# A seven-batch x ring in a tuned attention kernel: memory found by smaller buffers, and a smaller lead for the K waves

## The chip, the cores and the metric

One core of one Trainium2 chip. The metric is the device time of one execution in microseconds (us), as the median of several runs. Two versions are called the same when they differ by less than 2%.

## The reference

Two independent attention problems, A and B, of the same size. Their outputs stand side by side.

```python
# x [16,144,448], k_cache and v_cache [16,16,512,256], wq [448,4096], wo [4096,448], all bf16
q = (x @ wq).reshape(16, 144, 16, 256).transpose(0, 2, 1, 3)
scores = jnp.einsum("bhqd,bhkd->bhqk", q, k_cache) * (256 ** -0.5)
p = softmax(scores)
o = jnp.einsum("bhqk,bhkd->bhqd", p, v_cache)
out = o.transpose(0, 2, 1, 3).reshape(16, 144, 4096) @ wo
# ... the same for B; concatenate([a, b], axis=-1)
```

## The kernel before

The kernel calls one (problem, batch, head) a *unit*. There are 512, of about 2 us each: units 0 to 255 are A, 256 to 511 are B. TensorE does for each unit its Q projection (ahead of time), the scores S (three units ahead), P·V, a matmul with ones that sums the rows of P, and pieces of the output projection.

All loads but a few at the start go through one DMA queue, issued by SyncE. A K *wave* brings the K of 16 units at once by a transposing DMA (4.19 MB), into a ring of 32 units. A V load brings two units (512 KB), into a ring of nine. x comes in groups of two or four batches, into a ring of six batches. The weights wq and wo of B replace those of A around unit 256. The order of the queue is planned when the program is built:

```python
NV, NX = 9, 6
MARGIN, HOLD, K_FIX = 1.0, 1.0, 2.4
# ...
for XG, (g0, g1) in enumerate(X_GROUPS):      # groups of x, by batch: (2,6) (6,10) ... (18,20) ...
    load(first_q[g0], (g1 - NX) * H - lq(NT) if g1 > NX else s_min, 1.3 + 0.55 * (g1 - g0), t_load_x, XG)
for W, (u0, u1) in enumerate(WAVES):
    last = u1 - 1 - KR
    load(u0 - ls(u0), last - ls(last) + 1 if last >= 0 else s_min, K_FIX + 0.97 * (u1 - u0), t_load_k, W)
```

The arguments of `load` are the step that needs the transfer, the first step at which its buffer is free, and the time that the planner allows for it. `K_FIX` is the fixed part of that time for a K wave: a smaller one lets the wave be placed later against V loads.

The sum of the rows of P goes through three engines. GpSimd adds twice, VectorE folds the upper half of the partitions onto the lower, and TensorE sums with ones, once for two units:

```python
def t_presum(U):
    def e1(g):      # GpSimd, first add
        return g.tensor_tensor(pp_sb[:, :, :], pt_sb[:, psl, 0:2, :], pt_sb[:, psl, 2:4, :], op=ALU.add)
    # ...
    dst, key = (ps_sb[:, sl, :], (("ps", sl), U)) if U < P0 else (p2_sb[:, :], ("p2", U))
    def e2(g):      # GpSimd, second add
        return g.tensor_tensor(dst, pp_sb[:, 0, :], pp_sb[:, 1, :], op=ALU.add)

def t_halves(U):    # VectorE, the fold
    def e(v):
        return v.tensor_tensor(ps_sb[p0:p0 + 64, sl, :], p2_sb[0:64, :], p2_sb[64:128, :], op=ALU.add)
```

VectorE also copies Q out of PSUM (`qt_sb<-qp_ps`) and normalises P·V (`ring<-ot_ps,rinv_sb`). The scheduler adds the waits that reads and writes of the same buffer make necessary.

## Time and profile before

| | before |
|---|---|
| median, lowest, highest | 1050.94, 1048.6, 1051.23 us (3 runs) |
| profiled run | 1052.7 us, of which the profile spans 1050.9: slower than each of the timed runs |
| TensorE, VectorE, ScalarE, GpSimd busy | 1031.5, 797.3, 794.2, 631.9 us |
| longest wait of TensorE | 6.0 us, for the K wave of unit 288 |

The lines themselves are in the prediction below. Three notes on reading them. In a list of waits the three numbers are the sum in us, how often it happened and the longest. In a timeline a line is its start, its length, the engine with its line of code, the operation, the tiles, and in brackets how long the engine stood idle just before it and what released it. A line of a window has its length, the busy time and instruction count of the five engines (TensorE, its weight loads, VectorE, ScalarE, GpSimd), then the granted clock of TensorE (1.00 is full), the DMA share and GB/s.

### The profile page before, as it was taken

What the parts mean: (1) busy time and instruction counts of PE and PEld (TensorE: products, weight loads), DVE (VectorE), ACT (ScalarE), POOL (GpSimd) and SP (SyncE); (2) the same over time, 40 slices, a digit from 0 to 9 for tenths busy, and PEclk for the clock granted to TensorE, in tenths of its full rate; (3) what the DMA queues carried; (4) which work ended last, traced back from release to release, by engine and by line L of the source; (5) the groups of instructions that cost most, each with busy time, mean ns of one, the idle gap of its engine ahead of it and who ended that gap; (6) DMA issues with size and microseconds to landing.
All of it is one profiled execution on the core that took longest, in us unless ns stands there. A gap on an engine that the chain in (4) does not pass through costs nothing.

```text
span 1050.9 us, 32573 instructions
## 1 busy us (share of the span) xinstructions
PE 1031.5 (98%) x12432; PEld 877.9 (84%) x12432; DVE 797.3 (76%) x2042; ACT 794.2 (76%) x2368; POOL 631.9 (60%) x1030
## 2 busy tenths in 40 slices
PE   8999999999999999999999799999999999999997
PEld 8999888888788888888887688888888888888885
DVE  5776787778777787787677668788787777788874
ACT  5877677778777777888766568787887777788785
POOL 3654556666566666666655456666666666666673
PEclk9999999999999999999999999999999999999999
DMA  9999999999999999999999999999999999999970
GB/s 320 362 325 318 302 268 248 283 282 291 295 294 303 273 283 238 296 286 298 260 295 337 250 288 292 290 282 294 273 264 270 295 285 294 264 273 287 288 235 13
DMA packets 590884, 294.11 MB, mean 280 GB/s; under 512 B 501440, under 2 KB 515904, under 8 KB 590720
## 3 DMA queue, kind: packets, MB, share of 16 engines
q1 hardware_dynamic: 590240, 291.72, 111.5%
q8 instruction: 100, 1.64, 0.6%
q14 instruction: 64, 0.52, 0.1%
q10 hardware_dynamic: 480, 0.23, 0.1%
HBM read 161.74 MB, written 4.13 MB: 158 GB/s over the span
## 4 chain that ended last, share of the span: by engine, by line
PE 90%; DMA 8%; SPq 2%; issue 0%; ACT 0%; DVE 0%; DVEq 0%; ACTq 0%
PE ot_ps L1219 23%; PE s_ps L1163 23%; PE qp_ps L1132 22%; PE op_ps L1335 18%; DMA kt_sb<-in_B_k_cache_dram 3%; DMA kt_sb<-in_A_k_cache_dram 2%; PE ot_ps L1235 2%; DMA wq_sb<-in_A_wq_dram 1%; DMA v_sb<-in_B_v_cache_dram 1%; PE qp_ps L1083 1%; PE s_ps L1083 1%; SPq L1053 1%; DMA wq_sb<-in_B_wq_dram 1%; PE qp_ps L1335 1%; DMA v_sb<-in_A_v_cache_dram 0%; SPq L981 0%
## 5 line engine op out<-in xcount | busy, mean ns | idle before, releaser
L1183 POOL TENSOR_TENSOR pp_sb<-pt_sb 128x288 f32<-128x288 bf16 x512 | 380.5, 743 | 305.1 <-ACT pt_sb L1173 290.3
L1173 ACT ACTIVATE pt_sb<-s_ps 128x288 bf16<-128x288 f32 x1024 | 364.5, 408 | 182.0 <-PE s_ps L1163 176.3
L1163 PE MATMUL s_ps<-qt_sb,kt_sb 128*128 128x144 bf16 x4096 | 340.3, 226 | 6.4 <-DMA kt_sb<-in_B_k_cache_dram 5.8
L1219 PE MATMUL ot_ps<-pt_sb,v_sb 128*128 128x144 bf16 x4096 | 340.2, 226 | 2.6 <-DMA v_sb<-in_B_v_cache_dram 1.4
L1163 PEld LDWEIGHTS s_ps<-qt_sb,kt_sb 128*128 128x128 bf16 x4096 | 288.3, 98 | 55.2 <-issue 6.3
L1256 ACT ACTIVATE rinv_sb<-ln_sb 64x144 f32<-64x144 f32 x928 | 298.3, 321 | 24.2
L1132 PE MATMUL qp_ps<-xt_sb,wq_sb 128*128 128x288 bf16 (+1 forms) x2368 | 300.8, 270 | 1.9 <-DMA wq_sb<-in_A_wq_dram 1.2
L1335 PE MATMUL op_ps<-wo_sb,ring 128*128 128x448 bf16 x1120 | 286.0, 353 | 0.0
L1188 POOL TENSOR_TENSOR p_sb<-pp_sb 128x144 f32<-128x144 f32 x464 | 227.3, 490 | 92.4 <-DVE ps_sb L1197 53.3
L1219 PEld LDWEIGHTS ot_ps<-pt_sb,v_sb 128*128 128x128 bf16 x4096 | 274.3, 98 | 3.6 <-DVE ps_sb L1197 3.1
L1132 PEld LDWEIGHTS qp_ps<-xt_sb,wq_sb 128*128 128x128 bf16 x2368 | 212.2, 98 | 77.1 <-DVE run_sb L1286 1.1
L1146 DVE CAST qt_sb<-qp_ps 128x576 bf16<-128x576 f32 x216 | 163.4, 757 | 140.1 <-PE qp_ps L1132 139.9
L1197 DVE TENSOR_TENSOR ps_sb<-p_sb 64x144 bf16<-64x144 f32 x464 | 241.5, 520 | 34.9 <-POOL p_sb L1188 16.1
L1271 DVE TENSOR_TENSOR ring<-ot_ps,rinv_sb 128x288 bf16<-128x288 f32 (+2 forms) x640 | 237.6, 387 | 18.6 <-ACT rinv_sb L1256 13.6
L1286 DVE TENSOR_REDUCE run_sb<-ot_ps 128x1 bf16<-128x144 f32 x560 | 144.9, 300 | 41.7 <-ACT rinv_sb L1243 26.6
L1335 PEld LDWEIGHTS op_ps<-wo_sb,ring 128*128 128x128 bf16 x1120 | 94.0, 98 | 20.7 <-issue 0.5
L1243 ACT ACTIVATE ln_sb<-ot_ps 128x144 f32<-128x144 f32 x232 | 67.9, 293 | 33.6 <-PE ot_ps L1235 26.8
L1235 PE MATMUL ot_ps<-ps_sb,ones 128*128 128x144 bf16 x280 | 63.3, 226 | 0.0
L1145 DVE CAST qt_sb<-qp_ps 128x288 bf16<-128x288 f32 x80 | 36.0, 450 | 4.1 <-PE qp_ps L1132 3.2
L1091 ACT ACTIVATE kt_sb<-qp_ps 128x512 bf16<-128x512 bf16 x48 | 28.9, 602 | 0.9 <-PE qp_ps L1083 0.9
L1235 PEld LDWEIGHTS ot_ps<-ps_sb,ones 128*128 128x128 bf16 x280 | 27.4, 98 | 1.1 <-DVE ps_sb L1197 1.1
L1188 POOL TENSOR_TENSOR ps_sb<-pp_sb 128x144 bf16<-128x144 f32 x48 | 23.5, 489 | 6.9 <-PE ot_ps L1235 0.3
(37 smaller groups left out, 162.5 us busy)
## 6 DMA issues: line engine op xcount, KB each, us to landing
v_sb<-in_A_v_cache_dram SPq DMA_DIRECT2D x128, 512.0 KB, 7.4
v_sb<-in_B_v_cache_dram SPq DMA_DIRECT2D x128, 512.0 KB, 7.5
v_sb<-in_A_k_cache_dram SPq DMA_DIRECT2D x22, 512.0 KB, 10.1
out_dram<-ost_sb SPq DMA_DIRECT2D x36, 112.0 KB, 6.3
wo_sb<-in_A_wo_dram SPq DMA_DIRECT2D x8, 448.0 KB, 7.4
wo_sb<-in_B_wo_dram SPq DMA_DIRECT2D x8, 448.0 KB, 8.3
wq_sb<-in_B_wq_dram SPq DMA_DIRECT2D x4, 768.0 KB, 10.1
wq_sb<-in_A_wq_dram SPq DMA_DIRECT2D x3, 768.0 KB, 9.0
```

Source lines behind the costliest of these rows:

```text
L1132: ins = t.matmul(acc, lhsT=wq_sb[:, kc, c0:c0 + 128], rhs=xt_sb[:, kc, xo:xe + 1:max(xe - xo, 1), :], start=(kc == 0), stop=(kc == 3))
L1146: return v.tensor_copy(qt_sb[:, a:b + 1:b - a, :, :], qp_ps[:, :, 0:2 * SQ].rearrange("p e (u q) -> p u e q", u=2))
L1163: ins = t.matmul(s_ps[bank][:, (c % 2) * SQ:(c % 2 + 1) * SQ], lhsT=kt_sb[:, 2 * c + dc, ko:ko + 128], rhs=qt_sb[:, qsl, dc, :], start=(dc ...
L1173: return a.activation(pt_sb[:, psl, 2 * k:2 * k + 2, :].rearrange("p b q -> p (b q)"), s_ps[bank][:, 0:2 * SQ], AF.Exp, scale=DH ** -0.5)
L1183: return g.tensor_tensor(pp_sb[:, :, :], pt_sb[:, psl, 0:2, :], pt_sb[:, psl, 2:4, :], op=ALU.add)
L1188: return g.tensor_tensor(dst, pp_sb[:, 0, :], pp_sb[:, 1, :], op=ALU.add)
L1197: return v.tensor_tensor(ps_sb[p0:p0 + 64, sl, :], p2_sb[0:64, :], p2_sb[64:128, :], op=ALU.add)
L1219: ins = t.matmul(ot_ps[ob][:, dc * SQ:(dc + 1) * SQ], lhsT=v_sb[:, vsl, j, c * DH + dc * 128:c * DH + (dc + 1) * 128], rhs=pt_sb[:, sl, c, ...
L1256: return a.activation(rinv_sb[p0:p0 + 64, sl, :], ln_sb[h0:h0 + 64, :], AF.Exp, scale=-1.0)
L1271: ins = v.tensor_tensor(ring[:, 2 * h:2 * h + 2, r0:r0 + q1 - q0], ot_ps[ob][:, 0:2 * SQ].rearrange("p (c q) -> p c q", c=2)[:, :, q0:q1], ...
L1286: return v.tensor_reduce(run_sb[:, k, j:j + 1], ot_ps[ob][:, 2 * SQ:3 * SQ], axis=AX.X, op=op)
L1335: ins = t.matmul(acc[0:m, 0:D], lhsT=ring[:, c, col0:col0 + m], rhs=wo_sb[:, c, :], start=(c == op_first), stop=(c == op_last))
```

## The change

The intent: give x a ring of seven batches, so that x groups can be issued sooner and need not queue up beside K and V; issue one group 40 units sooner still; and place K waves with a smaller lead. The memory for the seventh batch comes from other buffers.

```diff
-    NV, NX = 9, 6
+    NV, NX = 9, 7
-    MARGIN, HOLD, K_FIX = 1.0, 1.0, 2.4
+    MARGIN, HOLD, K_FIX = 1.0, 1.0, 2.0
-        ps_sb = sb("ps_sb", [128, NPS, SQ], BF16)          # NPS = 2
+        ps_sb = sb("ps_sb", [128, SQ], BF16)
-        p2_sb = sb("p2_sb", [128, SQ], F32)
...      (short reductions in groups of 20 instead of 28, their results in bf16, a flag moved into another buffer)
-            dst, key = (ps_sb[:, sl, :], (("ps", sl), U)) if U < P0 else (p2_sb[:, :], ("p2", U))
+            dst, key = ps_natural(U) if U < P0 else (pp_sb[:, 0, :], ("pp", ("p2", U)))
...
-                return v.tensor_tensor(ps_sb[p0:p0 + 64, sl, :], p2_sb[0:64, :], p2_sb[64:128, :], op=ALU.add)
+                return v.tensor_tensor(ps_sb[p0:p0 + 64, :], pp_sb[0:64, 0, :], pp_sb[64:128, 0, :], op=ALU.add)
...
-                load(first_q[g0], (g1 - NX) * H - lq(NT) ...
+                load(first_q[g0] - (40 if g0 == Bn + 2 else 0), (g1 - NX) * H - lq(NT) ...
```

So the second add now writes into `pp_sb`, its own input, and the fold reads it there: the first add of the next unit must wait until the fold is done.

More of the change, by code (lines that the diff above doesn't have):

```diff
@@ L802, in bass_concat_heads__mha_block_cached__gqa_block_cached__near_ridge_kernel @@
     WARM = 32
-    NQT, NPT, NPS, NRI, NOST = 11, 4, 2, 2, 2
+    NQT, NPT, NRI, NOST = 11, 4, 2, 2
     RS = 3
@@ L812, in bass_concat_heads__mha_block_cached__gqa_block_cached__near_ridge_kernel @@
     NCK = P0 + (NT - P0) // 2
-    NRUN = max(n for n in range(1, 33) if NCK % n == 0)
+    NRUN = max(n for n in range(1, 21) if NCK % n == 0)
     assert P0 % KG == 0
@@ L841, in bass_concat_heads__mha_block_cached__gqa_block_cached__near_ridge_kernel @@
         pp_sb = sb("pp_sb", [128, 2, SQ], F32)
-        ps_sb = sb("ps_sb", [128, NPS, SQ], BF16)
+        ps_sb = sb("ps_sb", [128, SQ], BF16)
         rinv_sb = sb("rinv_sb", [128, NRI, SQ], F32)
-        p2_sb = sb("p2_sb", [128, SQ], F32)
         ln_sb = sb("ln_sb", [128, SQ], F32)
         run_sb = sb("run_sb", [128, 2, NRUN], BF16)
-        runs_sb = sb("runs_sb", [128, 2, NCK // NRUN], F32)
+        runs_sb = sb("runs_sb", [128, 2, NCK // NRUN], BF16)
         ost_sb = sb("ost_sb", [128, NOST, D], BF16)
-        stat = sb("stat", [128, 4], F32)
-        flag_sb = sb("flag_sb", [128, 4], I32)
+        stat = sb("stat", [128, 8], F32)
+        flag_sb = stat.bitcast(I32)[:, 4:8]
         qp_ps = ps("qp_ps", [128, 2, 512], F32)
@@ L957, in e @@
                     sems["wo%d" % wg], 16)
-            over = [(("xn", g), 1) for g in range(NX) if pr == 0 and wg in x_rows(g)[2]]
+            over = [(("xn", g), 1) for g in X_AT if pr == 0 and wg in x_rows(g)[2]]
             S.add(SP, e, writes=[(("wo", wg), pr)] + over, dma_sem="wo%d" % wg, name="wo%d.%d" % (pr, wg))
@@ L997, in x_rows @@
             n = SQ // XR
-            c0 = NWO - (NX - g) * n
+            c0 = NWO - (len(X_AT) - g) * n
             return n, wo_sb[0:XR, c0:c0 + n, :], sorted(set(c // WOG for c in range(c0, c0 + n)))
@@ L1176, in t_s, with ps_natural @@
                       name="ex%d.%d" % (U, k))
+        def ps_natural(U):
+            if U % 2:
+                return ost_sb[:, 1, 0:SQ], (("ost", 1), ("ps", U))
+            return ps_sb[:, :], ("ps", U)
         def t_presum(U):
             psl = U % NPT
-            sl = U % NPS
             def e1(g):
@@ L1191, in t_halves @@
         def t_halves(U):
-            sl = U // 2 % NPS
             p0 = U % 2 * 64
             def e(v):
-                return v.tensor_tensor(ps_sb[p0:p0 + 64, sl, :], p2_sb[0:64, :], p2_sb[64:128, :], op=ALU.add)
-            S.add(DVE, e, reads=[("p2", U)], writes=[(("ps", sl), ("p", U // 2)), ("halves", U)], name="hv%d" % U)
+                return v.tensor_tensor(ps_sb[p0:p0 + 64, :], pp_sb[0:64, 0, :], pp_sb[64:128, 0, :], op=ALU.add)
+            S.add(DVE, e, reads=[("pp", ("p2", U))], writes=[("ps", ("p", U // 2)), ("halves", U)], name="hv%d" % U)
         def ring_cols(pr, b):
@@ L1228, in t_sum @@
             if U < P0:
-                rhs, keys = ps_sb[:, U % NPS, :], [("ones", 0), (("ps", U % NPS), U)]
-            else:
-                sl = U // 2 % NPS
-                rhs, keys = ps_sb[:, sl, :], [("ones", 1), (("ps", sl), ("p", U // 2))]
+                rhs, key = ps_natural(U)
+                keys = [("ones", 0), key]
+            else:
+                rhs, keys = ps_sb[:, :], [("ones", 1), ("ps", ("p", U // 2))]
             def e(t):
@@ L1451, in load_list @@
             for XG, (g0, g1) in enumerate(X_GROUPS):
-                load(first_q[g0], (g1 - NX) * H - lq(NT) if g1 > NX else s_min, 1.3 + 0.55 * (g1 - g0), t_load_x, XG)
+                load(first_q[g0] - (40 if g0 == Bn + 2 else 0), (g1 - NX) * H - lq(NT) if g1 > NX else s_min, 1.3 + 0.55 * (g1 - g0), t_load_x, XG)
             for W, (u0, u1) in enumerate(WAVES):
```

## The prediction

> **What bounds the kernel now.** I read the page's busy shares first, then the list of waits of TensorE, then the chain of waits around the longest of them, then the DMA queue's own timeline with the landing time of every transfer.
>
> ```profile
> PE 1031.5 (98%) x12432; PEld 877.9 (84%) x12432; DVE 797.3 (76%) x2042; ACT 794.2 (76%) x2368; POOL 631.9 (60%) x1030
> ...
> PE s_ps L1163 <- DMA kt_sb<-in_B_k_cache_dram: 5.8, 1, 5.8
> PE ot_ps L1219 <- DMA v_sb<-in_B_v_cache_dram: 1.4, 2, 1.2
> PE ot_ps L1219 <- DMA v_sb<-in_A_v_cache_dram: 1.2, 1, 1.2
> PE qp_ps L1132 <- DMA wq_sb<-in_A_wq_dram: 1.2, 2, 0.9
> ```
>
> TensorE is busy 98% of 1050.9 us, and the change takes no matmul away. So only its waits can be won. Comparing each matmul's start-to-start time with the usual one for its form (62 ns for 144 columns, 123 for 288, 189 for 448) gives all that TensorE loses after its first matmul: 14.5 us. After the ramp the losses that matter, by position, are 0.5 at 181 us (K wave for unit 80), 1.4 at 266 (V of unit 120), 0.7 at 521 (first wq of B), 1.3 at 561 (V of unit 268), 6.0 at 598 (K wave for unit 288), 0.4 at 758 (V of unit 364). All are waits for a transfer.
>
> ```profile
> 573.05 4.24 SPq L1053 DMA_DIRECT2D v_sb<-in_B_v_cache_dram  x4
> 577.33 24.43 SPq L1039 DMA_TRANSPOSE kt_sb<-in_B_k_cache_dram  x1
> 601.80 0.58 SPq L1364 DMA_DIRECT2D out_dram<-ost_sb  x1
> ...
> 597.42 0.23 PE L1235 MATMUL ot_ps<-ps_sb,ones 128*128 128x144 bf16 x1
> 597.49 0.54 PE L1335 MATMUL op_ps<-wo_sb,ring 128*128 128x448 bf16 x2
> 603.87 1.12 PE L1163 MATMUL s_ps<-qt_sb,kt_sb 128*128 128x144 bf16 x8 [5.84 <-DMA kt_sb<-in_B_k_cache_dram]
> 604.78 1.16 PE L1219 MATMUL ot_ps<-pt_sb,v_sb 128*128 128x144 bf16 x8
> 605.74 1.70 PE L1335 MATMUL op_ps<-wo_sb,ring 128*128 128x448 bf16 x4
> ...
> 598.00:610.00 12.00, 6.16 (x46) 4.65 (x46) 2.49 (x7) 2.73 (x9) 2.09 (x4) 0.72 1.11 288
> ```
>
> The reader is to see three things. A transposed K wave of 16 units (4.19 MB) holds the one queue for 24 us: nothing behind it is issued until it is nearly done. Four V loads go out just before it. And after the 6 us gap the next matmuls run slow (8 in 1.12 us instead of 0.66) until about 608.4 us: some 2.8 us more. The stall costs 8.8 us, over half of all that can be won.
>
> **What the Trainium skill says.** "TensorE: Matmul & The Clock Gate", section "Why this matters for your kernels": keep idle gaps under about 3 us, else the clock falls to half. The trace agrees: 0.72 granted clock in the window above, and no slow matmuls after the 1.4 us gaps. "DMA: Bandwidth & Descriptors", section "Latency and other measured facts", gives a transposing DMA 261 GB/s; here a wave lands 17.1 us after the transfer ahead of it (median of those with a queue), 245 GB/s, against 1.35 us for a V load of 512 KB, 388 GB/s. "SBUF — State Buffer", section "SBUF: two separate sides": a VectorE operation with two SBUF inputs and a GpSimd operation that reads SBUF exclude each other, and the loser waits. The trace agrees, with the fold of the row sums on VectorE:
>
> ```profile
> 704.37 0.73 POOL L1183 TENSOR_TENSOR pp_sb<-pt_sb 128x288 f32<-128x288 bf16 x1 [0.76 <-ACT pt_sb L1173]
> 704.49 0.78 DVE L1197 TENSOR_TENSOR ps_sb<-p_sb 64x144 bf16<-64x144 f32 x1
> 705.35 0.49 POOL L1188 TENSOR_TENSOR p_sb<-pp_sb 128x144 f32<-128x144 f32 x1 [0.24 <-DVE ps_sb L1197]
> 705.87 0.30 DVE L1197 TENSOR_TENSOR ps_sb<-p_sb 64x144 bf16<-64x144 f32 x1
> ```
>
> **The change, part one: smaller buffers.** The room for a seventh batch comes from one ps_sb instead of two and from folding in place in pp_sb. Each engine's instructions keep their order, but for 8 more short reductions on VectorE (14 groups of 20 instead of 10 of 28; at about 0.1 us each, nothing). New waits: GpSimd's first add of unit U+1 waits for VectorE's fold of U, and an even fold for the sum matmul of the pair before. In the window above the add at 704.37 would wait for the fold at 704.49, which now runs alone in 0.30 us: it starts at about 704.83, and its fold ends at 706.5 instead of 706.17. VectorE then has 0.5 us of reductions before the Q eviction at 707.13, ahead of which it idles 0.45 us today. The 0.3 us fit into that. The sum matmul that the even fold waits for ended at 701.94, before the fold's start at 702.08. So TensorE sees nothing. VectorE gains: 464 folds of 520 ns mean become about 305 ns, some 100 us less busy, off the path. I put +0.2 us on it.
>
> **Part two: the order of the queue.** The queue's order in both built programs shows few moves: K waves 2 and 16 ahead of one V load each, K wave 3 ahead of x group 1 and two V loads; ten V loads (units 120, 252, 362, 394 and six others) ahead of a K wave; V loads of units 266, 330 and 378 behind one; x groups 2, 3, 4 and 7 one place earlier, each now ahead of a K wave that it followed. The x group issued 40 units sooner moves from unit 220 to 204.
>
> Working by landing times of the kernel before, with a load's own cost taken off or put on:
> - Unit 80: the wave lands 17.1 us after 158.7, at 175.8, no wait: -0.5. But V of unit 76 now follows wave and x; after wave 7 with x group 2 the V landed 5.1 us behind the wave (298.5, 303.6), so 180.9 against a use at 179.2: +1.7.
> - Unit 120: its V goes ahead of the wave: -1.4.
> - First wq of B: V of unit 252 goes ahead of that wave, so wq lands 1.35 later: wait 2.1 instead of 0.7.
> - V of unit 266 now behind its wave: lands 1.4 before where V of unit 268 landed (562.3), 560.9; use at 557.0 + 1.4 = 558.4: wait 2.6 in place of 1.3 at unit 268.
> - Unit 288: one V load behind the wave, which lands 1.35 sooner, 602.3. TensorE arrives at 597.8 + 1.4 + 1.3 = 600.5: wait 1.8 instead of 6.0, too short for the slow clock (-2.8).
> - Unit 300: its V landed at 635.1, and no byte ahead of it has gone; x group 5, cut at a batch of the ring, becomes two transfers, say +0.7: 635.8. TensorE, now 7.0 - 2.7 = 4.3 ahead of 636.6, would arrive at 632.3: a new wait of 3.5. Net from units 256 to 300: -0.8.
> - Unit 364: same bytes ahead, unchanged. Unit 378: V lands about 786.3 against 785.2: +1.0.
>
> Sum: -0.5 + 1.7 - 1.4 - 0.8 + 1.0 + 0.2 = +0.2, so 1051. The reason that so large a wait gives so little: from the first wq of B the queue is never empty, with 8 wq transfers and 8 wo loads (3.4 us a pair and 1.2 each, 23 us in all) on top of the usual 30 us in each 31 us of matmuls. Moving a load inside a full queue moves the wait; only shortening the queue removes it.
>
> **The rivals.** *The queue gets shorter*: x groups 3 and 4 (5.1 and 2.4 us between landings) go where the queue may have slack. For it: wave 11 took 19.6 us, the least of all, so it had nothing ahead, and V loads were then 25 to 28 us early. Against it: landings 1.35 us apart right up to it, and waves 12 and 13 with 6 us ahead of them. If 2.4 us of queue go, each wait from 521 to 636 us shrinks by as much, and the gain at unit 300 stays: 1047; with x behind wave 3 landing in time as well, 1044. *The plan holds*: all waits listed but the start and the 112 us one go, -0.5 - 1.4 - 0.7 - 1.3 - 8.8 - 0.4, and none comes: 1038. *VectorE becomes late*: the fold loop of two units takes about 2 x (0.73 + 0.49 + 0.30 + 0.2) = 3.4 us against 3.8 us of matmuls; where a step has no output-projection pair (0.38 us less) the slack is used up. If one pair in three lost 0.1 us over 232 pairs, +8: 1059. The 0.45 us idle before the Q eviction speaks against it.
>
> **Range and chances.** My sum is 1051; I give the shorter queue a weight of about a third and move to 1049. Low 1042: the shorter queue and no new wait at 76, 266 and 378. High 1053: each new wait a third larger. Over 2% faster would be under 1029.9, below even the 1038 with every listed wait gone, so 0.02. Over 2% slower, 1072, needs a VectorE loop that stalls throughout: 0.02.
>
> **What would show it.** Right: the wait for K at unit 288 under 3 us with no slow matmuls after; V waits near units 76, 266 and 300; V of unit 120 on time; folds at about 305 ns and VectorE near 700 us busy; matmul counts unchanged. Wrong: no wait at unit 300 (the queue did get shorter, time near 1043); a wait at 288 as long as before (the V behind it did not matter); TensorE waiting for VectorE or GpSimd in many short pieces.

## The result, and the profile after

The changed kernel ran in 1056.66 us (median of 4 runs, 1055.7 to 1058.01), beside 1050.12 us (median of 4) of the kernel before. The ratio is 1.0064, with a 95% interval from 1.0046 to 1.0083: 0.6% slower, within the 2% called the same, but above the predicted range of 1042 to 1053. A ratio here is the mean time of one kernel's fast runs over the mean of the other's in the same rounds (in the experiments without the first run of each), so it is not quite the ratio of the medians quoted.

The page of the changed kernel, busy time by engine:

```profile
PE 1034.7 (98%) x12432; PEld 879.3 (83%) x12432; DVE 706.8 (67%) x2050; ACT 794.5 (75%) x2368; POOL 623.8 (59%) x1030
```

Its list of waits, the four lines that matter:

```profile
POOL pp_sb L1186 <- DVE ps_sb L1199: 241.0, 348, 2.2
...
PE ot_ps L1221 <- DMA v_sb<-in_B_v_cache_dram: 8.5, 4, 4.2
...
PEld s_ps L1162 <- DVE qt_sb L1144: 5.5, 10, 1.0
...
PE qp_ps L1131 <- DMA wq_sb<-in_B_wq_dram: 2.7, 1, 2.7
```

The matmuls are the same 12432. VectorE is 90 us less busy. The 5.8 us wait for a K wave is gone from the list. In its place stand four waits for V and a longer one for wq of B, and two kinds that the kernel before hardly has: GpSimd's first add waits 348 times for the fold of VectorE (new), and the weight loads of S wait ten times for a Q copy of VectorE. The waits of GpSimd cost nothing by themselves. Those of S do.

**Where the time went.** I matched the start of each unit's P·V in the two traces. The differences (after less before, in us) by stretch of units, from the two profiled runs (1050.9 and 1056.2 us):

| units | change in the stretch | difference at its end | what is seen there in the changed kernel's trace |
|---|---|---|---|
| 0 to 8 | -1.2 | -1.2 | the first loads, whose order is the same; over all traces the difference here goes from -1.2 to +1.1 |
| 8 to 232 | -2.2 | -3.4 | waits at units 80 (0.5) and 120 (1.4) gone (see below) |
| 232 to 240 | +0.64 | -2.76 | S waits for VectorE |
| 248 to 252 | +3.45 | +0.69 | wait of 2.9 for the first wq of B, then slow matmuls |
| 264 to 268 | +4.67 | +5.37 | wait of 4.4 for V of unit 266, then slow matmuls |
| 268 to 272 | +0.39 | +5.76 | S waits for VectorE |
| 272 to 288 | -8.7 | -2.97 | no wait at unit 288, no slow matmuls |
| 296 to 304 | +4.16 | +1.19 | wait of 2.5 for V of unit 300, then slow matmuls |
| 304 to 488 | +2.0 | +3.21 | V of 346, 364 and 378 (1.5) |
| 488 to 511 | +2.13 | +5.35 | S waits for VectorE, seven times |

By cause: VectorE 0.64 + 0.39 + 2.13 = 3.2; transfers from unit 304 on 2.0; the start and the queue up to unit 304 together 5.35 - 3.2 - 2.0 = 0.2. In this pair all that was won early was lost again: TensorE came 2.8 us earlier to the first wq of B and left that wait 0.7 us later than before.

**How far one trace goes.** A trace is one execution, and the waits for transfers differ between executions with the same order of the queue. The runs e1, e5 and d2 below have the order of the kernel before up to the first wo of B, yet none of them waits at unit 80, and at unit 120 they wait 0, 0.1 and 0.6 us, against 0.5 and 1.4 us in the kernel before. The changed kernel, e7 and d1 have one order up to there too; they wait 2.9, 6.6 and 0.1 us for the first wq of B, which landed at 521.7, 525.8 and 519.4. So the rows on units 80 and 120 and on the first wq describe this pair, and that the new order caused them is not shown. Two things do repeat. One is the trade at units 266, 288 and 300: with the lead of before (before, e1, e3, e5, e8) the wait at unit 288 is 5.2 to 6.2 us, and there is none at 300; with the new lead (the changed kernel, e2, e6, e7) there is none at 288, but 1.9 to 4.4 us at 266 and 2.5 to 4.8 at 300. The other is the waits for VectorE: all five traces with the fold in place (the changed kernel, e1, e3, e6, d1) lose 0.45 us at unit 272 and seven times 0.3 at units 496 to 508, four of them 0.7 at unit 240; in the other traces these places lose at most 0.3 us together.

**The wait for VectorE.** The timeline of the kernel before, at the S of unit 243:

```profile
496.51 0.79 POOL L1183 TENSOR_TENSOR pp_sb<-pt_sb 128x288 f32<-128x288 bf16 x1
...
497.45 0.49 POOL L1188 TENSOR_TENSOR p_sb<-pp_sb 128x144 f32<-128x144 f32 x1
...
497.97 0.30 DVE L1197 TENSOR_TENSOR ps_sb<-p_sb 64x144 bf16<-64x144 f32 x1 [0.68 <-POOL p_sb L1188]
...
498.19 0.52 DVE L1286 TENSOR_REDUCE run_sb<-ot_ps 128x1 bf16<-128x144 f32 x2
...
498.63 0.45 DVE L1145 CAST qt_sb<-qp_ps 128x288 bf16<-128x288 f32 x1
...
499.13 0.49 PEld L1163 LDWEIGHTS s_ps<-qt_sb,kt_sb 128*128 128x128 bf16 x8 [0.31 <-DVE qt_sb L1145]
```

The same place in the changed kernel, which is 3.40 us ahead until then:

```profile
493.36 0.31 DVE L1199 TENSOR_TENSOR ps_sb<-pp_sb 64x144 bf16<-64x144 f32 x1 [0.31 <-POOL pp_sb L1191]
...
493.81 0.73 POOL L1186 TENSOR_TENSOR pp_sb<-pt_sb 128x288 f32<-128x288 bf16 x1 [0.48 <-DVE ps_sb L1199]
...
494.62 0.49 POOL L1191 TENSOR_TENSOR pp_sb<-pp_sb 128x144 f32<-128x144 f32 x1
...
495.21 0.30 DVE L1199 TENSOR_TENSOR ps_sb<-pp_sb 64x144 bf16<-64x144 f32 x1 [1.06 <-POOL pp_sb L1191]
...
495.44 0.51 DVE L1288 TENSOR_REDUCE run_sb<-ot_ps 128x1 bf16<-128x144 f32 x2
...
495.87 0.44 DVE L1144 CAST qt_sb<-qp_ps 128x288 bf16<-128x288 f32 x1
...
496.37 0.67 PE L1162 MATMUL s_ps<-qt_sb,kt_sb 128*128 128x144 bf16 x8 [0.51 <-DVE qt_sb L1144]
```

Take 3.40 off the times before. The first add would start at 493.11; now it waits for the fold of the unit before and starts at 493.81, 0.70 late. The second add comes at 494.62 instead of 494.05, the fold at 495.21 instead of 494.57, the Q copy at 495.87 instead of 495.23, and S at 496.37 instead of 495.73: all 0.6 late. The key is the last line before: there the weight load of S already waited for the Q copy, so the copy had no slack, and its whole delay lands on TensorE. VectorE itself stands idle for 1.06 us ahead of the fold. It is late because it is told to wait in order, not because it is full.

At units 496 to 508 it is a loop that repeats. Add, add, fold and the next first add now follow one another. From the same timeline, further on:

```profile
1020.71 0.73 POOL L1186 TENSOR_TENSOR pp_sb<-pt_sb 128x288 f32<-128x288 bf16 x1 [0.55 <-ACT pt_sb L1172]
...
1022.48 0.73 POOL L1186 TENSOR_TENSOR pp_sb<-pt_sb 128x288 f32<-128x288 bf16 x1 [0.48 <-ACT pt_sb L1172]
...
1023.29 0.49 POOL L1191 TENSOR_TENSOR pp_sb<-pp_sb 128x144 f32<-128x144 f32 x1
...
1023.88 0.30 DVE L1199 TENSOR_TENSOR ps_sb<-pp_sb 64x144 bf16<-64x144 f32 x1 [1.05 <-POOL pp_sb L1191]
...
1024.33 0.73 POOL L1186 TENSOR_TENSOR pp_sb<-pt_sb 128x288 f32<-128x288 bf16 x1 [0.55 <-DVE ps_sb L1199]
```

(Two of the adds are put down to ScalarE; each starts 0.15 us after the fold before it ended, like the one put down to VectorE.) Two units take 1024.33 - 1020.71 = 3.62 us. TensorE's pace there, from one pair of P·V to the next, was 3.32 us in the kernel before; it is 3.62 in the changed kernel and in e1, and 3.32 again in e5 and e7, which take the wait away.

The fold itself did what was hoped. Before and after, from the costliest groups (busy us, mean ns of one):

```profile
L1197 DVE TENSOR_TENSOR ps_sb<-p_sb 64x144 bf16<-64x144 f32 x464 | 241.5, 520 | 34.9 <-POOL p_sb L1188 16.1
```

```profile
L1199 DVE TENSOR_TENSOR ps_sb<-pp_sb 64x144 bf16<-64x144 f32 x464 | 141.3, 304 | 159.0 <-POOL pp_sb L1191 124.8
```

**The wait at unit 300.** The timeline of the changed kernel, first of the queue, then of TensorE, and its window line:

```profile
604.26 23.84 SPq L1038 DMA_TRANSPOSE kt_sb<-in_B_k_cache_dram  x1
628.14 3.10 SPq L980 DMA_TRANSPOSE xt_sb<-in_B_x_dram  x2
631.29 2.20 SPq L1052 DMA_DIRECT2D v_sb<-in_B_v_cache_dram  x4
...
633.12 0.66 PE L1162 MATMUL s_ps<-qt_sb,kt_sb 128*128 128x144 bf16 x8
636.13 0.66 PE L1221 MATMUL ot_ps<-pt_sb,v_sb 128*128 128x144 bf16 x8 [2.35 <-DMA v_sb<-in_B_v_cache_dram]
...
632.00:640.00 8.00, 5.65 (x54) 4.46 (x52) 3.51 (x13) 3.98 (x12) 3.64 (x6) 0.82 1.05 349
```

The V load at 631.29 stands behind a K wave and an x group. It landed at 636.0; in the kernel before it landed at 635.1, and TensorE came to it at 636.6, after it. Now TensorE is there 2.5 us before it lands. The stall at unit 288 is gone, and a stall of half its size (4.2 us with its slow matmuls, against 8.4) stands here. After it the granted clock is 0.82.

### The profile page after: what moved, and what is told of

Read it like the earlier page. It is cut to its first block, busy times and chain, and to the rows that moved or that the text cites. A ratio compares the mean times of both kernels' runs of the same rounds, so it can differ in the third digit from the quotient of the medians.

```text
span 1056.2 us, 32350 instructions
## 1 busy us (share of the span) xinstructions
PE 1034.7 (98%) x12432; PEld 879.3 (83%) x12432; DVE 706.8 (67%) x2050; ACT 794.5 (75%) x2368; POOL 623.8 (59%) x1030
## 4 chain that ended last, share of the span: by engine, by line
PE 90%; DMA 3%; POOL 2%; SPq 2%; DVE 1%; ACT 1%; issue 1%; POOLq 0%; DVEq 0%; ACTq 0%
PE qp_ps L1131 23%; PE ot_ps L1221 23%; PE s_ps L1162 22%; PE op_ps L1337 19%; DMA v_sb<-in_B_v_cache_dram 2%; PE ot_ps L1237 2%; DMA wq_sb<-in_A_wq_dram 1%; POOL pp_sb L1186 1%; PE qp_ps L1082 1%; PE s_ps L1082 1%; POOL pp_sb L1191 1%; DMA wq_sb<-in_B_wq_dram 1%; PE qp_ps L1337 1%; SPq L980 1%; DVE ps_sb L1199 0%
## 5 line engine op out<-in xcount | busy, mean ns | idle before, releaser
L1186 POOL TENSOR_TENSOR pp_sb<-pt_sb 128x288 f32<-128x288 bf16 x512 | 373.0, 728 | 376.0 <-DVE ps_sb L1199 241.0
L1191 POOL TENSOR_TENSOR pp_sb<-pp_sb 128x144 f32<-128x144 f32 x464 | 226.6, 488 | 36.4
L1199 DVE TENSOR_TENSOR ps_sb<-pp_sb 64x144 bf16<-64x144 f32 x464 | 141.3, 304 | 159.0 <-POOL pp_sb L1191 124.8
L1237 PE MATMUL ot_ps<-ps_sb,ones 128*128 128x144 bf16 x256 | 58.0, 226 | 0.0
L1237 PEld LDWEIGHTS ot_ps<-ps_sb,ones 128*128 128x128 bf16 x256 | 25.1, 98 | 0.0
L1090 DVE COPY kt_sb<-s_ps 128x512 bf16<-128x512 bf16 x48 | 20.0, 416 | 2.7 <-PE s_ps L1082 2.3
```

The costliest lines, as they stand in the source:

```text
L1199: return v.tensor_tensor(ps_sb[p0:p0 + 64, :], pp_sb[0:64, 0, :], pp_sb[64:128, 0, :], op=ALU.add)
```

## The experiments

Theories at the start. **A**: the fold in place makes VectorE late; it costs what the waits for it show. **B**: the smaller lead of the K waves (K_FIX) costs, by V loads that come late. **C**: the x groups placed by the ring of seven cost. Later: **D**: between the first wq of B and unit 300 the queue is full, and sets when TensorE leaves that stretch; time won before it comes back as waits inside it. In what follows a wait is what TensorE lost at one place by the distance of its matmuls' starts, slow matmuls after it not counted, so it is 0.15 to 0.2 us above the gap in a list of waits. One question needed no run: with the 40 units taken out again the program built is the same instruction for instruction on every engine. That group goes where the ring of seven lets it go, with or without the 40.

**e1_buffers**: the changed kernel with the ring, the lead and the x group of before. Only the buffers are changed.

```diff
-    NV, NX = 9, 7
+    NV, NX = 9, 6
-    MARGIN, HOLD, K_FIX = 1.0, 1.0, 2.0
+    MARGIN, HOLD, K_FIX = 1.0, 1.0, 2.4
-                load(first_q[g0] - (40 if g0 == Bn + 2 else 0), ...
+                load(first_q[g0], ...
```

> The smaller buffers alone: one ps_sb, the fold in place in pp_sb, six batches of x and the old lead, so that the queue of transfers is in the order of the kernel before. Theory A (VectorE late behind GpSimd costs TensorE time where Q of one batch alone is evicted, units 240 to 256 and 496 to 511): +2 to +3 us, waits of TensorE for the Q eviction there, the K wait at unit 288 as long as before. Theory B (all of the loss is the order of the queue): within 0.5 us of before.

Measured: 1052.06 us (1051.0 to 1056.15) beside 1050.41; ratio 1.0027 [1.0009, 1.0046]. The queue's order is that of before and the K wait at unit 288 is 6.2 us, but S waits for VectorE as in the changed kernel. The buffers alone cost about 2.8 us.

**e2_lead**: the kernel before with the smaller lead alone.

```diff
-    MARGIN, HOLD, K_FIX = 1.0, 1.0, 2.4
+    MARGIN, HOLD, K_FIX = 1.0, 1.0, 2.0
```

> The smaller lead of K waves alone, on the kernel before (all buffers and six batches as before). Theory B (order of the queue): +2.5 to +4 us; waits at the first wq of B, at units 266 and 300 and 378 as in the changed kernel, none of 6 us at unit 288, no wait for VectorE. Theory A: 0 to -3 us, as the waits at units 80 and 120 go and nothing takes their place.

Measured: 1051.18 us (1048.14 to 1053.95); ratio 1.0001 [0.9983, 1.0020]. Theory B falls in this form. The wait at unit 288 is gone; in its place stand 1.0 (wq of B), 3.5 (V of 266), 2.7 (V of 300), 1.9 (V of 346) and 0.9 us (V of 378), with 1.7 and 1.6 of slow matmuls after the second and third. In this trace one is traded for the other. The waits of S for VectorE are those of the kernel before (0.3 us in all).

**e3_oldlead**: the changed kernel with the lead of before.

```diff
-    MARGIN, HOLD, K_FIX = 1.0, 1.0, 2.0
+    MARGIN, HOLD, K_FIX = 1.0, 1.0, 2.4
```

> The changed kernel with the old lead: seven batches and small buffers, but V of units 266, 286, 330, 378 ahead of their K waves again. Theory A: +2 to +3 us with the 6 us wait at unit 288 back and no wait at units 300 and 378. Theory B: within 1 us of before. If moving the x groups matters by itself (theory C: x ahead of waves 10 and 12 fills the queue before the burst of wq and wo), the wait at the first wq of B is 2 us or more here too.

Measured: 1054.31 us (1051.36 to 1058.0); ratio 1.0040 [1.0019, 1.0061]. The waits for VectorE are there (0.67, 0.45 and 2.07 at the same units), the K wait at unit 288 is back (5.9 and 2.4 of slow matmuls), and the V of unit 120 costs 2.8 and 1.7 of slow matmuls. Most of the loss seems to stay without the smaller lead, though the intervals overlap.

**e5_own_fold**: e1 with the separate fold buffer back, so that the first add need not wait for the fold. The single `ps_sb` and all else stay.

```diff
+        p2_sb = sb("p2_sb", [128, SQ], F32)
-            dst, key = ps_natural(U) if U < P0 else (pp_sb[:, 0, :], ("pp", ("p2", U)))
+            dst, key = ps_natural(U) if U < P0 else (p2_sb[:, :], ("p2", U))
-                return v.tensor_tensor(ps_sb[p0:p0 + 64, :], pp_sb[0:64, 0, :], pp_sb[64:128, 0, :], op=ALU.add)
+                return v.tensor_tensor(ps_sb[p0:p0 + 64, :], p2_sb[0:64, :], p2_sb[64:128, :], op=ALU.add)
```

> As e1_buffers, but the half sums have a tensor of their own again, so that GpSimd's next first add does not wait for VectorE's fold; ps_sb stays single. If the fold in place is what makes VectorE late: the loss of e1_buffers is gone, 0 to +0.5 us. If the single ps_sb is (the even fold waits for the sum matmul): the same as e1_buffers.

Measured: 1050.71 us (1049.77 to 1051.94); ratio 1.0008 [0.9993, 1.0023], in the same rounds as e1. The waits of S for VectorE in e1, then in e5:

```profile
PEld s_ps L1162 <- DVE qt_sb L1144: 5.5, 10, 0.9
```

```profile
PEld s_ps L1163 <- DVE qt_sb L1145: 0.8, 3, 0.5
```

Of what TensorE lost to them (0.68 + 0.45 + 2.07 = 3.2 us in e1's trace) 0.3 is left in e5's. The time fell by 0.19%, 2.0 us, though the two intervals overlap. It is the fold in place, not the single `ps_sb`.

**e6_oldx**: the changed kernel with the ring of seven, but the x groups placed as a ring of six would allow.

```diff
-                load(first_q[g0] - (40 if g0 == Bn + 2 else 0), (g1 - NX) * H - lq(NT) if g1 > NX else s_min, ...
+                load(first_q[g0] - (40 if g0 == Bn + 2 else 0), (g1 - 6) * H - lq(NT) if g1 > 6 else s_min, ...
```

> The changed kernel with seven batches and small buffers and the new lead, but each x group may be placed only as soon as a ring of six would allow; the queue is then in the order of e2_lead but for one V load. Theory C (x groups 3, 4 and 7 placed earlier, ahead of K waves, cost what is left of the loss): the loss falls from 6.5 us to that of e1_buffers, +2.5 to +3.5 us over before; the wait at the first wq of B falls from 2.9 to about 1 us. If the loss comes of buffers and lead together and not of the x groups: +5.5 to +7, as the changed kernel.

Measured: 1057.92 us (1056.32 to 1061.33) beside 1052.2; ratio 1.0059 [1.0040, 1.0079]. Nothing is won back that can be seen: 1.0059 against 1.0064 (of other rounds). Theory C falls in this form.

**e7_twopp**: the changed kernel with `pp_sb` in bf16 and two buffers of it, the same bytes; the first add no longer waits for the fold of the unit just before. The result is still correct.

```diff
-        pp_sb = sb("pp_sb", [128, 2, SQ], F32)
+        pp_sb = sb("pp_sb", [128, 2, 2, SQ], BF16)
-                return g.tensor_tensor(pp_sb[:, :, :], ...
+                return g.tensor_tensor(pp_sb[:, U % 2, :, :], ...
```

> The changed kernel, with the first sums in bf16 in two buffers of the same bytes in all, so that GpSimd's next first add doesn't wait for VectorE's fold; queue order exactly that of the changed kernel. Theory A: the waits for the Q eviction at units 240 to 256 and 496 to 511 go and the loss falls by 2.5 to 3 us, to about +4 over before. If the fold's wait is not the cause, +6.5 remains.

Measured: 1055.28 us (1052.32 to 1057.31), in the same rounds as e6; ratio 1.0025 [1.0004, 1.0046], where the changed kernel has 1.0064. So 0.39%, 4.1 us, went with the waits for VectorE, of which 0.3 us is left; the changed kernel's ratio is of other rounds. This is theory A again, by another way. Its trace also has waits of 6.6 us for the first wq of B and 4.8 us for V of unit 300. They are no sign of D: TensorE is 0.4 us later at unit 248 than in the changed kernel's trace, not earlier, and the wq landed 4.1 us later with the same order of the queue.

**b1** and **b2**: the kernel before with loads moved by hand to where they seemed best. In b1, K wave 3 goes ahead of x group 1, V of unit 120 ahead of its wave, K wave 16 ahead of one V load, and x groups 5 and 6 behind others. In b2 also the first wq of B goes ahead of K wave 14.

```diff
+        move(t_load_k, (3,), t_load_x, (1,))
+        move(t_load_k, (6,), t_load_v, (60,), True)
+        move(t_load_k, (16,), t_load_v, (143,))
+        move(t_load_x, (5,), t_load_k, (18,))
+        move(t_load_x, (6,), t_load_k, (22,))
+        move(t_load_wq, (1, 0), t_load_k, (14,))       # b2 only
```

> A trial at a better kernel: the kernel before, with five moves in its queue and nothing else: K wave 3 ahead of x group 1, V of unit 120 ahead of wave 6, V of unit 286 behind wave 16, x groups 5 and 6 just ahead of the next K wave instead of just behind one. If what counts at unit 300 is when the queue gets to its V load (theory D): that lands 1.8 us sooner for x 5 moved out of its way, so -2 to -4 us in all. If the moves only shift waits, within 1 us of before.

> As b1, and the first wq of B ahead of K wave 14. Theory D: the wait at the first wq of B (0.7 us) goes, wave 14 lands about 3 us later, which its 6.7 us of slack allow; as the V load of unit 300 is no sooner for it, the same time as b1 within 0.5 us. If each wait counts by itself, 0.7 us or more below b1.

Measured: b1 1068.1 us, ratio 1.0154 [1.0136, 1.0172]; b2 1067.8 us, ratio 1.0145 [1.0124, 1.0166]. Both were spoiled by my x moves. Q is projected for batches in pairs, so these groups are needed earlier than I took: TensorE waited 8.3 and 5.6 us for x in b1, 10.6 and 6.4 in b2. They say nothing on D.

**d1_after_shortwo** and **d2_before_shortwo**: Their outputs are wrong, which doesn't matter for the times. The wo loads of B bring a quarter of their bytes, in the changed kernel (d1) and in the one before (d2). This shortens the full queue and nothing else.

```diff
-                return q.dma_start(wo_sb[:, c0:c0 + WOG, :],
+                n = 1 if pr else WOG
+                return q.dma_start(wo_sb[:, c0:c0 + n, :],
```

> Wrong result on purpose: the changed kernel, with each of the eight wo loads of B cut to a quarter (112 of 448 KB), which takes about 8 x 0.9 = 7.2 us out of the queue between wave 15 and wave 16. Theory D (from the first wq of B to unit 300 the end is set by when the full queue gets there): the wait at V of unit 300 (2.5 us and some 0.8 of slow clock, 4.2 us against the kernel before at that unit) goes, so 3 to 4 us less than the changed kernel, about +3 over before; the waits at the first wq and at unit 266, which lie ahead of the cut, stay. If each wait is set by its neighbours in the queue alone, unit 300 still waits.

> Wrong result on purpose: the same cut in the kernel before. Theory D: K wave 16 lands 7 us sooner, so that the wait of 6 us at unit 288 and its 2.8 us of slow clock go: -7 to -9 us. If the place of the V load of unit 286 is what matters there: no more than -2.

Measured in the same rounds, before 1050.68: d1 1050.07 us, ratio 0.9991 [0.9954, 1.0028]; d2 1044.28 us, ratio 0.9942 [0.9901, 0.9983]. By medians, d2 is 6.4 us below the kernel before, and d1 is at -0.6 where the changed kernel is at +6.5, so some 7 us lower. The wait at unit 300 is gone in d1, that at unit 288 in d2. The waits for VectorE in d1 stay (0.68, 0.45, 2.12). This part of D is shown by d2 and fits d1: bytes taken out of the full stretch are time won. But d1 won twice the 3 to 4 us that was expected, and part of that is not the cut's: the wait for the first wq of B lies ahead of the cut and was to stay, and it is 0.1 us in this trace. d1 stays 5 to 6 us above d2. The intervals are wide (0.4% each way), so these sizes are rough.

**b3_actq**: the kernel before with wq and wo of B issued from ScalarE's queue, to unload the full one.

```diff
-            S.add(eng, e, writes=[(("wq", h), pr) for h in range(h0, h1)], ...
+            S.add(ACT if pr else eng, e, writes=[(("wq", h), pr) for h in range(h0, h1)], ...
-            S.add(SP, e, writes=[(("wo", wg), pr)] + over, ...
+            S.add(ACT if pr else SP, e, writes=[(("wo", wg), pr)] + over, ...
```

> A trial at a better kernel: the kernel before, with the wq and wo loads of B issued from ScalarE's queue in place of SyncE's, at the same places of the program, so that they no longer stand behind a K wave in the one queue and the gap after each wave is filled. Theory D: the queue is shorter by the gaps, the waits at 521, 561 and 598 us shrink, -3 to -8 us. If the two queues only share the same rate: the K waves they run beside land later, within 2 us of before; if issuing costs ScalarE much (16 issues of some 0.5 us), exps come late and it is slower.

Measured: 1068.35 us (1063.08 to 1073.91); ratio 1.0153 [1.0115, 1.0192]. One wait of 24 us, and no other for a transfer of any size after it. The queue's issue of K wave 14, and the wait:

```profile
494.75 49.30 SPq L1039 DMA_TRANSPOSE kt_sb<-in_B_k_cache_dram  x1
```

```profile
548.69 1.12 PE L1219 MATMUL ot_ps<-pt_sb,v_sb 128*128 128x144 bf16 x8 [24.11 <-DMA v_sb<-in_A_v_cache_dram]
```

The wave was issued at 494.8 and landed at 546.1; the four wq transfers of 896 KB (1024 bytes each) were issued at 499.8 to 522.7 and landed at 511.9 to 542.5. The last V load ahead of the wave landed at 501.2, so 4.19 + 3.67 = 7.86 MB took 44.9 us, about 175 GB/s; the profile's own windows show 148 to 183 GB/s between 505 and 545 us, where the kernel before moves 239 to 330 between 500 and 550. One after the other, by the durations used in the prediction, they would take 17.1 + 4 x 3.4 = 30.7 us. The V load stands behind the wave, which issued for 49 us instead of 22, and comes when the wave has landed. The Trainium skill ("DMA: Bandwidth & Descriptors", section "Rules for kernel authors") says that spreading DMAs over several issuing engines does not help bandwidth, because they interleave on the same DMA engines. The run agrees, and more: the rate falls to 175 GB/s from the 256 that the same bytes in 30.7 us would give. Why it falls is not settled by this run.

**e8_twopp_oldlead**: e7 with the lead of before, so that the ring of seven, its x order and the single `ps_sb` are what is left.

```diff
-    MARGIN, HOLD, K_FIX = 1.0, 1.0, 2.0
+    MARGIN, HOLD, K_FIX = 1.0, 1.0, 2.4
```

> The changed kernel with the two bf16 buffers of e7 and the old lead: of the change, only seven batches, the x groups that follow from it, and the single ps_sb stay. A least-squares fit of the six ratios so far to three costs that add up gives +0.36% for the fold in place, +0.14% for the lead and +0.10% for the x groups: +0.10%, about 1 us over before. If the three don't add up (the x groups need the new lead to do harm): 0; if x is the larger part: +0.25% or more.

Measured: 1053.15 us (1051.05 to 1056.92); ratio 1.0018 [0.9987, 1.0050]. No loss to VectorE over 0.3 us, a K wait of 5.8 at unit 288. The interval holds zero and half of the whole loss: inconclusive on x and lead. For the fold it gives a third pair: e3 has the same order of the queue, with the fold in place, and 1.0040; the difference is 0.22%, 2.3 us (other rounds, overlapping intervals).

**b4_threemoves**: what b1 should have been, the first three moves alone.

```diff
+        move(t_load_k, (3,), t_load_x, (1,))
+        move(t_load_k, (6,), t_load_v, (60,), True)
+        move(t_load_k, (16,), t_load_v, (143,))
```

> The kernel before with three moves in the queue and nothing else: K wave 3 ahead of x group 1 (takes off the wait of 0.5 us at unit 80), V of unit 120 ahead of its wave (1.4 us), K wave 16 ahead of one of the four V loads before it (it lands 1.35 us sooner). It is the run that b1 should have been, without the two x moves that spoiled it. Theory D (the full queue from the first wq of B to unit 300 sets when TensorE gets there, so time won before it comes back as waits inside it): the waits at units 80 and 120 go, unit 256 is reached at nearly the same time as before because the wq wait grows from 0.7 to about 2.5 us, and the time is -1.5 to +1 us against the kernel before. Rival (each wait is worth its own length): -0.5 - 1.4 - 1.4 and less of the slow clock, that is 3.3 to 6 us faster.

Measured: 1048.69 us (1047.56 to 1049.95) beside 1049.42; ratio 0.9995 [0.9981, 1.0009], that is 0.5 us by the ratio. The rival's 3.3 us (0.31%) lie outside the interval. This does not decide for D, though: 1.9 of the 3.3 us are the waits at units 80 and 120, which e1 and e5 hardly have either, with the order of before, so there was less to win than I took; and the interval (2.0 us faster to 0.9 slower) leaves room for the 1.4 us of the third move. Nor is the mechanism of D in the trace. The waits for K and V of B:

```profile
PE s_ps L1163 <- DMA kt_sb<-in_B_k_cache_dram: 4.4, 1, 4.4
PE ot_ps L1219 <- DMA v_sb<-in_B_v_cache_dram: 2.3, 2, 1.6
```

The waits at units 80 and 120 are gone, but the wq wait did not grow in this trace; the wait at unit 288 is 4.4 instead of 5.8 (as in the lists), V of 346 costs 1.8, and V of 364 nothing instead of 0.4. The profiled run was the fastest of the six. So that the time hardly moved is measured; why is not. It does not beat the kernel before by more than the interval, and no other version does: the best kernel that computes the right result stays the one before, with b4 level.

## Why the prediction was wrong

**The bound was right.** TensorE's waits were all there was to win or lose; the matmuls are the same and TensorE is at 98% in both.

**The step that failed: "So TensorE sees nothing ... I put +0.2 us on it."** The measured cost of the fold in place is 3.2 us by the trace, 2.0 us by e1 against e5, 2.3 by e3 against e8 and 4.1 by the changed kernel against e7 (the last two across rounds; each pair has one order of the queue). The dependence was named rightly ("GpSimd's first add of unit U+1 waits for VectorE's fold of U"), and so was the rival ("*VectorE becomes late*"). What failed is the choice of window. I took one, at 704 us, where Q is copied for two batches at once and VectorE idles 0.45 us ahead of the copy. Near units 240 to 272 and 496 to 511 Q of a single batch is copied, right ahead of its S. At units 238, 240 and 494 the slack was already zero: in the profile before, the weight load of S starts 0.05 us after the Q copy ends, and the line at 499.13 shows it waiting. At units 496 to 507 it was 0.2 to 0.5 us. All this was there before the prediction. And at 496 to 508 the rival's own sum was close: it put the loop of two units at 3.4 us against 3.8 of matmuls, less 0.38 where there is no output-projection pair. Measured are 3.62 us (the gaps between the instructions are larger than the 0.2 allowed for a unit) against 3.32. The prediction set this sum aside because of the 0.45 us idle in its one window.

**VectorE's gain was right and worthless**: folds at 304 ns against 305 predicted, 706.8 us busy against "near 700". The Trainium skill ("SBUF — State Buffer", section "SBUF: two separate sides") says that the loser of the pair waits; the traces agree: before, 442 of the 464 folds overlap a GpSimd add, now none does, and the mean fell from 520 to 304 ns. The sequence that brought this about is also what made VectorE late.

**The queue, term by term** (predicted against measured in the profiled pair):

| place | predicted | measured |
|---|---|---|
| unit 80 | -0.5 | -0.5, but also gone in e1, e5 and d2 without the new order |
| V of unit 76 | lands 180.9, +1.7 | 0: it landed at 176.4, 1.6 us ahead of its use |
| V of unit 120 | -1.4 | -1.4, but also 0, 0.1 and 0.6 left in e1, e5 and d2 |
| first wq of B | lands 523.7, wait 2.1 | landed 521.7, wait 2.9 and slow matmuls, +3.45 in all |
| V of unit 266 | lands 560.9, wait 2.6 | landed 562.0, wait 4.4 and slow matmuls, +4.67 |
| unit 288 | wait 1.8 | none: the wave landed at 601.8 (602.3 predicted), TensorE came later |
| unit 300 | lands 635.8, wait 3.5 | landed 636.0, wait 2.5, and slow matmuls |
| unit 378 | +1.0 | +1.5 |

The landing times from unit 266 on were good to about a microsecond; the wq was 2.0 us earlier than worked out and V of 76 4.5 earlier. The hits at units 80 and 120 are at least in part luck, as three runs have them without the change. Three sizes were wrong. First, slow matmuls follow the new waits of 2.5 to 4.4 us; I had counted them only for the wait at unit 288, and there as 2.8 us, where the distances of the starts give 2.35. Second, the wait at V of 76 did not come. Third, TensorE reached the wq wait 2.8 us earlier, not 0.2 as my early terms add up to, and so waited longer though the wq landed sooner. To the end of unit 304 the sums are nevertheless close, which with errors both ways is luck too: -0.5 + 1.7 - 1.4 - 0.8 = -1.0 predicted and 0.2 measured. The sentence "Moving a load inside a full queue moves the wait; only shortening the queue removes it" has support in its second half from d2 (6.4 us) and d1. Its first half is what the traces show at units 266, 288 and 300, and e2 (0.0%) fits it. From unit 304 on, 1.0 was predicted and 2.0 measured.

**The lean to 1049 was wrong.** The sum itself was 1051. The wait at unit 300, which I had named as the sign against a shorter queue, was there. The high end of the range, "each new wait a third larger", gave VectorE no room at all, though I had named it a rival at +8 us; that is the second half of the same error.

**Open.** e1 puts about 2.8 us of the 6.5 on the buffers. The remainder, for lead and x order, comes out as 0 (e2), 2 (e8) and 2.6 us (e7), each with some 2 us or more of uncertainty; which of the two it is, the runs do not settle. Nor do the parts add up: e6 has the order of e2 but for one V load and x groups cut in other places, and the buffers of e1; those cost 0.01% and 0.27% alone, e6 costs 0.59%. The runs were on different chips, so this may be an effect of both together, of the seventh batch, or of the chip. That is the part of the prediction's miss, some 3 us, whose cause stays open.

## What to carry to other kernels

When a buffer is shared between two engines to save memory, ask at every kind of step, not at one typical one, whether the instruction that comes after it in the engine's order has slack; a weight load or matmul that already waits for that engine by a few tenths of a microsecond is the warning. A busy time that falls is not a gain when the engine now idles in order. And where one queue is full for a long stretch, count its bytes: in d2 taking bytes out won time, and no reordering tried here did by more than its interval; a second queue beside a transposing transfer can make both slower. Before a wait in one trace is taken as a gain to be had, look for it in a second execution: the waits at units 80 and 120 were not in three others.

## What the Trainium skill lacked or had wrong

- "TensorE: Matmul & The Clock Gate", section "Why this matters for your kernels": idle gaps over about 3 us bring the lower clock. The length of the gap does not decide it here. In the changed kernel a wait of 2.35 us was followed by slow matmuls (granted clock 0.82, shown above). In e8 a wait with 3.3 us lost (at 264.9 us) and in e6 one with 3.5 us lost (at 520.7 us) were not; their windows:

```profile
264.00:272.00 8.00, 4.89 (x57) 3.90 (x56) 3.56 (x9) 3.53 (x11) 2.92 (x5) 1.00 0.96 328
```

```profile
520.00:528.00 8.00, 4.62 (x55) 3.64 (x53) 2.85 (x9) 2.99 (x9) 2.58 (x5) 1.00 1.05 352
```

  The same page (Part 1) says that its window of activity runs freely, which would fit; no run here shows the window. Losses of 1.5 to 1.9 us (e1, e2, e5, b4) brought no slow matmuls.
- "DMA: Bandwidth & Descriptors" lacks what plain loads from a second queue do to a transposing load: about 175 GB/s for both together in b3, against 245 GB/s for a wave and 388 for a V load by itself.
- The same page lacks that a transposing transfer holds the issue of its queue: 17 to 28 us for the waves of 4.19 MB in the changed kernel's trace, until 2.0 to 4.3 us before they land. The first V load behind a wave mostly lands 1.2 to 2.8 us after it in the changed kernel's trace.
- "SBUF — State Buffer" was right on the shared side (fold 520 and 304 ns). No page says what it costs to avoid the collision by making one engine wait: 2.0 to 4.1 us here, by three pairs of runs.
